# Attention, layer norm and a float32 feed-forward on one core: the first pass's stores begun from GpSimd's queue, the residual stored in token order

## The chip, the cores and the metric

The kernel runs on one core of a Trainium2 chip. The metric is the device time of one execution in microseconds (us); the median of several runs is compared. TensorE is written PE, VectorE DVE, ScalarE ACT, GpSimd POOL and SyncE SP. A DMA is begun by an instruction on the queue of one of these engines (SP, ACT, or POOL) and then runs by itself.

## What is computed

```python
# q, k, v: (8, 8, 576, 64) float32; x below is (8, 576, 512), heads side by side
q_d, k_d, v_d = mean over each 4 tokens            # 144 pooled tokens
out_up  = repeat(softmax(scale * q_d @ k_d.T) @ v_d, 4)          # pooled attention
out_loc = softmax(scale * q @ k.T where |i - j| < 4) @ v         # local attention
x  = out_up + out_loc
xn = (x - mean(x)) / sqrt(var(x) + 1e-6) * g_ln                  # over 512 columns
return x + relu(xn @ w_ch1) @ w_ch2                              # 512 -> 2048 -> 512
```

The weights arrive as 8-byte floats, which the kernel reads as pairs of 32-bit words and turns into float32 itself. Each float32 product of the feed-forward is made of three faster ones, from a high and a low part of either operand.

## The kernel before

**Work.** The 4608 tokens of the 8 batches are cut in two ways. Attention goes by *windows*: window `i` (40 in all, 5 to a batch) holds two rows of 58 queries (56 in a batch's last window), `par` 0 and 1, each inside a stretch of 64 rows. The feed-forward goes by *chunks* of 512 tokens, 9 in all. Its 2048 hidden columns are split in two sets: a first pass visits all 9 chunks with the first set (5 pairs of 256 columns, plain products, line 1224 up and 1295 down), a second pass visits them again with the second set (3 pairs, a form with 7 products for 8, line 1214 up). Attention and norm of all windows run beside the first pass, so the first pass is where loads, pooling and norms are; the second pass has only the feed-forward.

**What goes through DRAM.** The first pass stores four things. `ud` (line 963): pooled attention of half the heads of a batch, each row written 4 times, 2 DMAs, read back by windows as `up` (line 1021). `xs` (line 1091): the residual x of a window, as it stands in SBUF, all 128 rows with the overlap of the windows, 1 DMA. `blocks` (line 1131): the normalised, transposed operand of a chunk, 4 DMAs, read back in the second pass (line 1146). `parts` (line 1364): the first pass's share of the output, 128 tokens to a DMA, after ACT has evicted it from PSUM (line 1361). In the second pass `fetch` brings `xs` and `parts` back for 128 tokens at a time; since `xs` lies by windows, the 128 rows are put together from 2 to 4 DMAs (line 1388), `parts` from one (line 1385). POOL adds the two (line 1391), DVE adds the second pass's share out of PSUM (line 1394), SP stores the result (line 1399).

**The engines beside PE.** POOL pools raw q, k and v over 4 tokens (lines 827 and 828: `raw5q` gives half of `qd`; 5 is 2 times the batch plus the half of the heads), adds `up` to the window's local attention (line 1040), takes a power for the norm (line 1053), and in the second pass makes sums of operands (line 1165) and line 1391. The raw tiles have two buffers in all, so a load waits until POOL has pooled the one before the last. PE turns `qd` and `kd` (line 875), makes pooled scores (902), turns the exponentials (921) and multiplies by the pooled v (938). SP begins the loads: raw tiles (line 814), windows of q and k in blocks (561, 4 DMAs to a task), windows of v (578 and 584), weights (359, 364). A block load of q or k may be given to ACT's queue instead (`alt` in `local`, windows from 16 on).

**The order.** Every piece of work is a task of a planner (`Plan`): an engine, a cost in us, what it depends on, a due time, and the buffers it takes and gives. `Plan.order` lists all tasks by a forecast of times and the kernel then emits them in that order, so each engine's instructions stand in a fixed order and an instruction that waits holds up all behind it on its engine. The planner counts at most 8 DMAs in flight (`lanes`) for all queues together. Costs, leads and due times are numbers in the kernel (`W_NORM`, `W2_LATER`, `DB` and others): when one changes, the order of every engine can change.

## Time and profile before

| what | value |
|---|---|
| median of 3 runs | 1067.28 us (1064.33 to 1073.89) |
| the profiled execution | 1064.17 us |
| its span, first to last instruction | 1062.5 us |
| mean granted clock of PE, as a share of full speed | 0.988 |
| instructions | 22984 |
| moved by DMA | 160.28 MB |

The profiled execution took 1064.17 us, of which 1062.5 us are the span; 1.7 us lie around it. Busy times are sums over an engine's instructions. Matmuls overlap and their ends are modelled, so a PE that is busy all the time can still be slowed; where PE stands still the timeline gives the idle time before an instruction in square brackets, with what ended it. "SPq" and "ACTq" rows are DMA-issuing instructions on a queue, with the time they took to issue; the transfer itself follows. Each row of a timeline is an instruction, or several equal ones in a row (x4), with start and length. The granted clock is 1.00 at 2.4 GHz and 0.50 at 1.2 GHz.

### The profile page before, as it was taken

What the parts mean: (1) busy time and instruction counts of PE and PEld (TensorE: products, weight loads), DVE (VectorE), ACT (ScalarE), POOL (GpSimd) and SP (SyncE); (2) the same over time, 40 slices, a digit from 0 to 9 for tenths busy, and PEclk for the clock granted to TensorE, in tenths of its full rate; (3) what the DMA queues carried; (4) which work ended last, traced back from release to release, by engine and by line L of the source; (5) the groups of instructions that cost most, each with busy time, mean ns of one, the idle gap of its engine ahead of it and who ended that gap; (6) DMA issues with size and microseconds to landing.
All of it is one profiled execution on the core that took longest, in us unless ns stands there. A gap on an engine that the chain in (4) does not pass through costs nothing. (4 is left out here: it accounts for less than half of the span.)

```text
span 1062.5 us, 22984 instructions
## 1 busy us (share of the span) xinstructions
PE 1021.6 (96%) x8330; PEld 861.6 (81%) x8330; DVE 663.7 (62%) x1573; ACT 434.7 (41%) x1352; POOL 363.8 (34%) x358
## 2 busy tenths in 40 slices
PE   9899999898999899999999999999998999999998
PEld 8678777777777688878888887888888999988897
DVE  6899874675565375655665554654646775466574
ACT  6686743362442354244453452553323223222221
POOL 4343454443534543352320111220213244214422
PEclk9999999999999999999999999999999999999999
DMA  7999877768787857667556242431345333433433
GB/s 177 226 270 243 205 171 164 185 164 177 165 174 177 190 132 188 139 171 186 144 136 167 75 132 81 139 120 55 105 128 170 103 108 108 159 124 105 131 118 119
DMA packets 284930, 160.28 MB, mean 151 GB/s; under 512 B 194704, under 2 KB 248080, under 8 KB 284816
## 3 DMA queue, kind: packets, MB, share of 16 engines
q1 hardware_dynamic: 263056, 156.18, 55.5%
q10 hardware_dynamic: 21760, 2.63, 1.7%
q8 instruction: 66, 1.08, 0.4%
q14 instruction: 48, 0.39, 0.1%
HBM read 111.68 MB, written 47.05 MB: 149 GB/s over the span
## 5 line engine op out<-in xcount | busy, mean ns | idle before, releaser
L1295 PE MATMUL acc<-hiw,hl 128*128 128x512 f32 x576 | 236.3, 410 | 4.9 <-ACT s L1252 2.5
L1295 PE MATMUL acc<-low,hh 128*128 128x512 f32 x576 | 226.5, 393 | 0.0
L1295 PE MATMUL acc<-hiw,hh 128*128 128x512 f32 x576 | 226.3, 393 | 0.0
L1295 PEld LDWEIGHTS acc<-hiw,hl 128*128 128x128 f32 x576 | 109.2, 190 | 27.8 <-ACT s L1252 3.1
L1295 PEld LDWEIGHTS acc<-hiw,hh 128*128 128x128 f32 x576 | 108.9, 189 | 24.3
L1232 ACT ACTIVATE hh<-h 128x256 fp32r<-128x256 f32 x180 | 59.6, 386 | 163.5 <-PE h L1224 99.9
L1295 PEld LDWEIGHTS acc<-low,hh 128*128 128x128 f32 x576 | 109.5, 190 | 17.4
L1391 POOL TENSOR_TENSOR back<-back,back 128x512 f32<-128x512 f32 x36 | 49.4, 1404 | 193.1 <-DMA back<-parts 170.1
L1239 DVE SCALAR_TENSOR_TENSOR hl<-h,hh 128x256 fp32r<-128x256 f32 x180 | 67.2, 414 | 76.6 <-ACT hh L1232 75.6
L1224 PE MATMUL h<-hix,hiw 128*128 128x512 f32 x360 | 111.0, 404 | 0.0
L1224 PE MATMUL h<-hix,low 128*128 128x512 f32 x360 | 103.1, 407 | 2.2 <-DVE low L408 0.8
L1224 PE MATMUL h<-lox,hiw 128*128 128x512 f32 x360 | 97.8, 394 | 0.0
L1040 POOL TENSOR_TENSOR xl<-xl,up 128x512 f32<-128x512 f32 x35 | 45.2, 1297 | 145.1 <-DVE xl L749 27.9
L1224 PEld LDWEIGHTS h<-lox,hiw 128*128 128x128 f32 x360 | 68.2, 189 | 15.2
L1224 PEld LDWEIGHTS h<-hix,low 128*128 128x128 f32 x360 | 65.7, 191 | 16.2 <-ACT hix L402 1.9
L1275 ACT ACTIVATE hh<-e 128x256 fp32r<-128x256 f32 x108 | 38.3, 408 | 97.2 <-DVE e L1256 55.5
L1224 PEld LDWEIGHTS h<-hix,hiw 128*128 128x128 f32 x360 | 65.5, 190 | 12.7
L1088 ACT ACTIVATE xg<-px,gain 128x58 f32<-128x58 f32 (+15 forms) x280 | 61.7, 380 | 6.9 <-PE px L1065 6.7
L1281 DVE SCALAR_TENSOR_TENSOR hl<-e,hh 128x256 fp32r<-128x256 f32 x108 | 54.3, 554 | 8.1 <-ACT hh L1275 7.1
L1256 DVE TENSOR_TENSOR e<-h,s 128x512 f32<-128x512 f32 x27 | 18.5, 684 | 47.7 <-PE h L1214 40.7
L1214 PE MATMUL h<-hiT,los 128*128 128x256 f32 x216 | 44.2, 287 | 3.6 <-ACT part L1361 3.0
L938 PEld LDWEIGHTS gv<-vd,agt 72*72 72x72 f32 x512 | 38.4, 146 | 9.8 <-ACT agt L931 3.6
(237 smaller groups left out, 1951.3 us busy)
## 6 DMA issues: line engine op xcount, KB each, us to landing
s<-in_moe_w_ch_dram SPq DMA_DIRECT2D x64, 256.0 KB
xs<-xl SPq DMA_DIRECT2D x40, 256.0 KB
blocks<-xg SPq DMA_DIRECT2D x36, 256.0 KB
parts<-part SPq DMA_DIRECT2D x36, 256.0 KB
xf_B<-blocks SPq DMA_DIRECT2D x36, 256.0 KB
back<-parts SPq DMA_DIRECT2D x36, 256.0 KB
out_dram<-back SPq DMA_DIRECT2D x36, 256.0 KB
up<-ud SPq DMA_DIRECT2D x70, 128.0 KB
```

The lines of the kernel that those rows point to most:

```text
L938: nc.tensor.matmul(y.pv[:, qh, h2], lhsT=y.at[kh][:, h2, qh * GH : (qh + 1) * GH], rhs=vd[:, kh, 2 * pr + h2], start=kh == 0, stop=kh == 1,)
L1040: nc.gpsimd.tensor_add(xl(), xl(), x.up)
L1088: nc.scalar.activation(to, at, AF.Copy, scale=gain[:, kc : kc + 1])
L1214: nc.tensor.matmul(side(*PLACE[e]), lhsT=wt[:, k], rhs=xx[:, k], start=n == 0, stop=n == 5)
L1224: nc.tensor.matmul(y.ps[fi], lhsT=wt[a][:, kc * P : (kc + 1) * P], rhs=xx[b], start=n == 0, stop=n == 3 * KC - 1)
L1232: nc.scalar.activation(hh[v, p, th][:, 256 * fi : 256 * fi + 256], side(fi, th), AF.Relu)
L1239: nc.vector.scalar_tensor_tensor(out=hl[v, p, th][:, fs], in0=side(fi, th), scalar=0.0, in1=hh[v, p, th][:, fs].bitcast(F32), op0=ALU.max, ...
L1256: nc.vector.tensor_add(two(y.e1), two(y.ps[1]), both(y.s))
L1275: nc.scalar.activation(hh[v, p, th][:, 256 * fi : 256 * fi + 256], place(th, fi), AF.Relu)
L1281: eng.scalar_tensor_tensor(out=hl[v, p, th][:, fs], in0=place(th, fi), scalar=0.0, in1=hh[v, p, th][:, fs].bitcast(F32), op0=ALU.max, op1= ...
L1295: nc.tensor.matmul(acc[v, th][j], lhsT=lt[:, ts], rhs=rt, start=p == 0 and fi == 0 and n == 0, stop=p == npr - 1 and fi == 1 and n == 2,)
L1391: nc.gpsimd.tensor_add(y.x, y.x, y.p)
```

## The change

The stores `ud`, `xs`, `blocks` and `parts` are begun on POOL's queue instead of SP's. `xs` is laid out by tokens: a window's store is cut into its two rows of queries (2 DMAs of 58 or 56 rows, without the overlap), and `fetch` reads 128 tokens with one DMA. The planner counts DMAs in flight that POOL began apart from the others (`soft`), and gives a start on POOL a cost (`BEGUN`). Five numbers of the planner change with it: `W_NORM`, `W2_LATER`, `DB`, and the costs of the loads of q, k and v by SP. The number of tasks stays.

```diff
@@ Plan.order
-                    if len(self.landed) >= self.lanes:
-                        at = max(at, self.landed[-self.lanes])
+                    landed = self.soft if t.eng == "POOL" else self.landed
+                    if len(landed) >= self.lanes:
+                        at = max(at, landed[-self.lanes])
+                    if t.eng == "POOL":
+                        at += t.dur / t.pieces
...
-    W_NORM, G_NORM = 4.0, 9.0
+    W_NORM, G_NORM = 2.0, 9.0
-    W2_LATER = 4.0
+    W2_LATER = 7.0
+    BEGUN = 1.0
-                    ts.append(add("SP", 1.9, lambda src=src, nm=nm, jb=jb: load_blocks(src, nm, jb, nc.sync), ts,
+                    ts.append(add("SP", 1.95, lambda src=src, nm=nm, jb=jb: load_blocks(src, nm, jb, nc.sync), ts,
-        vt = add("SP", 2.65 if by_pe else 1.33, load_v, (last_local.v[i % NVW],), due - 8.0, lag=LAT, kb=360,
+        vt = add("SP", 2.75 if by_pe else 1.42, load_v, (last_local.v[i % NVW],), due - 8.0, lag=LAT, kb=360,
@@ keep (ud), in pooled_pair
-                nc.sync.dma_start(
+                nc.gpsimd.dma_start(
-        t = add("SP", 0.74, keep, x.od_done, due, lag=LAT, kb=640, n=2, more=0.6)
+        t = add("POOL", 2 * BEGUN, keep, x.od_done, due, lag=LAT, kb=640, n=2, more=0.6)
-    xs = dram.tile([B * NWIN, P, DM], F32, tag="xs", bufs=1, name="xs")
+    xs = dram.tile([NT, DM], F32, tag="xs", bufs=1, name="xs")
@@ spill (xs), in norm
-            nc.sync.dma_start(xs[i], xl())
+            for par in range(2):
+                q0, n = queries(i, par)
+                r0 = row_of(i, par)
+                nc.gpsimd.dma_start(xs[q0 : q0 + n], xl()[r0 : r0 + n])
-        spilled[i] = add("SP", 0.41, spill, (t, kept), due + 2.0, give=U, lag=LAT, kb=256)
+        spilled[i] = add("POOL", 2 * BEGUN, spill, (t, kept), due + 2.0, give=U, lag=LAT, kb=256, n=2, more=2.0)
@@ save (blocks), in operands
-                    nc.sync.dma_start(blocks[c, kc], block[c, kc])
+                    nc.gpsimd.dma_start(blocks[c, kc], block[c, kc])
-                block_done[c, kc, "saved"] = add("SP", 0.41, save, [t], due + 10.0, give=U, lag=LAT, kb=256)
+                block_done[c, kc, "saved"] = add("POOL", BEGUN, save, [t], due + 10.0, give=U, lag=LAT, kb=256)
-    DB = 5.4
+    DB = 5.8
@@ finish: parts and the way back
-                nc.sync.dma_start(parts[n], y.p)
+                nc.gpsimd.dma_start(parts[n * P : (n + 1) * P], y.p)
-                for i, r0, r, m in pieces:
-                    nc.sync.dma_start(t[r : r + m], xs[i, r0 : r0 + m])
+                nc.sync.dma_start(t, src[n * P : (n + 1) * P])
-                parted[n] = add("SP", 0.41, keep, (t,), due + 1.0, give=U, lag=LAT, kb=256)
+                parted[n] = add("POOL", BEGUN, keep, (t,), due + 1.0, give=U, lag=LAT, kb=256)
```

**What it moves.** SP's instructions, at the loads of the raw tiles of batch 2's second half of heads (`raw5`). Before, stores of `ud` and `xs` stand between the loads (`qr`, `kr` are block loads of q and k):

```order
L561 DMA qr_2361<-in_q_dram 32x8x32 x4
L963 DMA ud_2492<-od_2403 288x1x256 x2
L814 DMA raw5q_2497<-in_q_dram 72x4x256
L561 DMA kr_2407<-in_k_dram 32x8x32 x4
L814 DMA raw5k_2535<-in_k_dram 72x4x256
L561 DMA qr_2545<-in_q_dram 32x8x32 x4
L1091 DMA xs<-xl_1451 128x512
L1091 DMA xs<-xl_1638 128x512
```

After, at the same loads, SP has loads alone:

```order
L819 DMA raw5q_2599<-in_q_dram 72x4x256
L566 DMA kr_2511<-in_k_dram 32x8x32 x4
L583 DMA vwin_79<-in_v_dram 64x8x64 x2
L566 DMA qr_2684<-in_q_dram 32x8x32 x4
L566 DMA kr_2726<-in_k_dram 32x8x32 x4
L819 DMA raw5k_2774<-in_k_dram 72x4x256
L819 DMA raw5v_2776<-in_v_dram 72x4x256
```

The stores have left SP, and the load of `raw5v` stands right behind that of `raw5k`. Over the whole program SP loses 36 + 36 + 40 + 28 stores and 76 of the 112 pieces of the way back, and gains 40 block loads that ACT had: 1135 instructions become 959.

POOL's instructions at the same place. Before, the second halves of `raw5q` and `raw5k` are pooled one after the other:

```order
L1053 TENSOR_TENSOR mv_2489<-mv_2489,neg_half 128x1
L827 TENSOR_TENSOR raw5q_2497<-raw5q_2497 72x4x128
L828 TENSOR_TENSOR qd_2429<-raw5q_2497 72x256
L827 TENSOR_TENSOR raw5k_2535<-raw5k_2535 72x4x128
L828 TENSOR_TENSOR kd_2476<-raw5k_2535 72x256
L827 TENSOR_TENSOR raw5v_2640<-raw5v_2640 72x4x128
```

After, eight starts of stores stand between them:

```order
L832 TENSOR_TENSOR raw5q_2599<-raw5q_2599 72x4x128
L833 TENSOR_TENSOR qd_2508<-raw5q_2599 72x256
L1099 DMA xs<-xl_1662 58x512 x2
L1099 DMA xs<-xl_1886 58x512 x2
L1099 DMA xs<-xl_2223 58x512 x2
L1139 DMA blocks<-xg_0_1220 128x512
L1139 DMA blocks<-xg_1_1222 128x512
L832 TENSOR_TENSOR raw5k_2774<-raw5k_2774 72x4x128
L833 TENSOR_TENSOR kd_2681<-raw5k_2774 72x256
```

Each start stands behind whatever its tile waits for, and `kd` behind them all. Over the whole program POOL gets 180 starts (80 `xs`, 36 `blocks`, 36 `parts`, 28 `ud`) to its 363 instructions.

ACT's instructions near the second product of batch 3's second half of heads. Before, a block load stands between the exponentials `ag` and the copy `agt` of their transpose:

```order
L915 ACTIVATE ag_1_4048<-gs_1_4005,gmx_1_4031 96x144 x3
L561 DMA qr_4085<-in_q_dram 32x8x32 x4
L931 COPY agt_1_0_4130<-gt_1_0_4098 72x3x2x48
L931 COPY agt_1_1_4134<-gt_1_1_4105 72x3x2x48
```

After, the nearest block load stands between two halves of a relu of the feed-forward:

```order
L936 COPY agt_0_1_3984<-gt_0_1_3965 72x3x2x48
L1240 ACTIVATE hh_0_0_4003<-h_0_0_3935 128x256
L1240 ACTIVATE hh_0_1_4005<-h_0_0_3935 128x256
L566 DMA qr_4041<-in_q_dram 32x8x32 x4
L1240 ACTIVATE hh_0_0_4003<-h_0_1_4009 128x256
```

The 20 block loads that ACT begins (80 DMAs) become 10 (40 DMAs).

## Rows read from the trace of the kernel before

**Rows 1.** The page: busy time of each engine, its share of the span, and the number of instructions.

```profile
PE 1021.6 (96%) x8330; PEld 861.6 (81%) x8330; DVE 663.7 (62%) x1573; ACT 434.7 (41%) x1352; POOL 363.8 (34%) x358
```

**Rows 2.** What PE waited for: instruction and line, released by; us in total, times, longest.

```profile
PE gq L875 <- POOL kd L828: 4.2, 3, 1.7
PE lt L706 <- ACT la L697: 3.5, 2, 2.4
PE gv L938 <- ACT agt L931: 3.1, 1, 3.1
PE gt L921 <- ACT ag L915: 3.1, 2, 1.7
PE h L1214 <- ACT part L1361: 3.0, 1, 3.0
PE gv L938 <- POOL vd L828: 2.2, 2, 1.6
```

**Rows 3.** Busy time by engine in the seven stretches where the granted clock was 0.50 (columns: stretch, length, busy PE, PEld, DVE, ACT, POOL, clock, DMA share, GB/s).

```profile
153.10:156.50 3.40, 3.40 (x21) 2.68 (x12) 2.09 (x6) 3.39 (x13) 0.00 (x0) 0.50 0.65 131
197.50:200.80 3.30, 3.30 (x11) 2.61 (x11) 1.73 (x6) 0.95 (x4) 0.00 (x0) 0.50 0.26 44
262.40:265.70 3.30, 3.30 (x41) 2.75 (x40) 2.91 (x11) 0.00 (x0) 0.00 (x0) 0.50 0.97 185
327.20:330.50 3.30, 3.30 (x13) 2.62 (x12) 0.76 (x2) 1.35 (x4) 0.00 (x0) 0.50 0.89 206
368.20:371.50 3.30, 3.30 (x38) 2.27 (x37) 0.00 (x0) 1.77 (x6) 2.00 (x3) 0.50 0.96 287
457.00:460.20 3.20, 3.20 (x11) 2.46 (x9) 0.77 (x2) 0.91 (x3) 0.00 (x0) 0.50 0.74 204
805.10:808.40 3.30, 3.11 (x14) 3.11 (x15) 3.30 (x7) 0.90 (x3) 0.00 (x0) 0.50 0.57 194
```

**Rows 4.** SP's queue in order of time, 140 to 175 us: start, us, what.

```profile
140.64 1.72 SPq L963 DMA_DIRECT2D ud<-od  x2
142.46 0.57 SPq L814 DMA_DIRECT2D raw5q<-in_q_dram  x1
143.08 2.71 SPq L561 DMA_DIRECT2D kr<-in_k_dram  x4
145.89 0.36 SPq L814 DMA_DIRECT2D raw5k<-in_k_dram  x1
...
167.98 4.22 SPq L1364 DMA_DIRECT2D parts<-part  x2
...
174.34 0.36 SPq L814 DMA_DIRECT2D raw6q<-in_q_dram  x1
```

**Rows 5.** PE in order of time: two instructions before which it stood still, with the idle time and what ended it.

```profile
152.34 0.28 PE L875 MATMUL gq<-ident,kd 72*128 72x72 f32 x1 [1.75 <-POOL kd L828]
...
805.29 0.80 PE L1214 MATMUL h<-hiT,los 128*128 128x256 f32 x2 [3.02 <-ACT part L1361]
```

**Rows 6.** The four stores on SP's queue, by line: count, ns to issue one (min/median/max), first and last start in us.

```profile
L1364 SPq DMA_DIRECT2D parts<-part x36: 319/356/580, 168.0 to 806.0; - x36
...
L1091 SPq DMA_DIRECT2D xs<-xl x40: 319/405/1430, 42.2 to 678.7; - x40
...
L963 SPq DMA_DIRECT2D ud<-od x28: 810/840/895, 74.6 to 615.4; - x28
...
L1131 SPq DMA_DIRECT2D blocks<-xg x36: 319/394/530, 65.8 to 691.7; - x36
```

**Rows 7.** The block loads that ACT's queue begins, in the same form.

```profile
L561 ACTq DMA_DIRECT2D qr<-in_q_dram x48: 317/328/1332, 166.3 to 453.6; - x48
L561 ACTq DMA_DIRECT2D kr<-in_k_dram x32: 317/330/1237, 218.2 to 572.2; - x32
```

**Rows 8.** ACT in order of time around three of them: start, us, what, and the idle time before it with what ended it.

```profile
258.90 1.88 ACTq L561 DMA_DIRECT2D qr<-in_q_dram  x4
260.83 0.69 ACT L931 COPY agt<-gt 72x288 f32<-72x288 f32 x2 [9.36 <-DMA kr<-in_k_dram]
...
300.04 0.91 ACT L915 ACTIVATE ag<-gs,gmx 96x144 f32<-96x144 f32 x3 [8.31 <-DMA qr<-in_q_dram]
...
324.90 0.66 ACT L1232 ACTIVATE hh<-h 128x256 fp32r<-128x256 f32 x2 [6.81 <-DMA qr<-in_q_dram]
```

**Rows 9.** Busy time by engine in a long stretch of the first pass (columns as in rows 3).

```profile
100.00:300.00 200.00, 184.91 (x1667) 150.64 (x1666) 131.44 (x346) 88.11 (x294) 94.39 (x93) 0.97 0.79 177
```

**Rows 10.** POOL's groups of instructions, its longest over a whole tile and its smallest: count, busy us, mean ns, idle before with what ended it.

```profile
L1391 POOL TENSOR_TENSOR back<-back,back 128x512 f32<-128x512 f32 x36 | 49.4, 1404 | 193.1 <-DMA back<-parts 170.1 <-DMA xf_B<-blocks 23.0
...
L1053 POOL TENSOR_TENSOR mv<-mv,neg_half 128x1 f32<-128x1 f32 x40 | 22.5, 571 | 44.3 <-DVE mv L1050 38.4 <-DMA s<-in_moe_w_ch_dram 5.8
```

**Rows 11.** What SP's queue waited for: the reads of the second pass (1385 `parts`, 1146 `blocks`, 1388 `xs`).

```profile
SPq L1385 <- DMA back<-xs: 28.2, 17, 2.9
...
SPq L1146 <- DMA back<-xs: 18.0, 10, 2.8
SPq L1388 <- DMA back<-xs: 15.8, 11, 2.6
```

**Rows 12.** POOL in order of time in the second pass.

```profile
957.60 5.49 POOL L1391 TENSOR_TENSOR back<-back,back 128x512 f32<-128x512 f32 x4 [22.98 <-DMA back<-parts]
963.04 1.29 POOL L1165 TENSOR_TENSOR xT<-xf_B,xf_B 128x512 f32<-128x512 f32 x1
```

More of the change, by code (lines that the diff above doesn't have):

```diff
@@ L39, in __init__ @@
         self.wire, self.lanes = 1.05, 8
-        self.landed = []
+        self.landed, self.soft = [], []
     def add(self, eng, dur, fn, deps=(), due=0.0, take=(), give=(), lag=None, ahead=1e9, alt=None, kb=0, n=1, more=0.1, late=None):
@@ L125, in order @@
                 for _ in range(t.pieces):
-                    if len(self.landed) >= self.lanes:
-                        at = max(at, self.landed[-self.lanes])
+                    landed = self.soft if t.eng == "POOL" else self.landed
[3 more added lines that the diff above has]
+                        at += t.dur / t.pieces
                     self.moved = max(self.moved, at + self.wire) + t.kb / t.pieces / self.rate
-                    self.landed.append(self.moved + t.more)
-                    last = max(last, self.landed[-1])
-                    at += t.dur / t.pieces
+                    landed.append(self.moved + t.more)
+                    last = max(last, landed[-1])
+                    if t.eng != "POOL":
+                        at += t.dur / t.pieces
                 t.end = at
@@ L179, in attention_then_ffn @@
     NT = B * S
-    NTILE = NT // P
     TPC = 2 * T // P
@@ L991, in pooled_pair @@
             return
-        t = add("SP", 0.74, keep, x.od_done, due, lag=LAT, kb=640, n=2, more=0.6)
+        t = add("POOL", 2 * BEGUN, keep, x.od_done, due, lag=LAT, kb=640, n=2, more=0.6)
         ud_done.setdefault(b, []).append(t)
     block, block_done, spilled = {}, {}, {}
-    xs = dram.tile([B * NWIN, P, DM], F32, tag="xs", bufs=1, name="xs")
-    parts = dram.tile([NTILE, P, DM], F32, tag="parts", bufs=1, name="parts")
+    xs = dram.tile([NT, DM], F32, tag="xs", bufs=1, name="xs")
+    parts = dram.tile([NT, DM], F32, tag="parts", bufs=1, name="parts")
     blocks = dram.tile([NCH, KC, P, 512], F32, tag="blocks", bufs=1, name="blocks")
@@ L1363, in keep, with fetch @@
             def keep(y=y, n=n):
-                nc.sync.dma_start(parts[n], y.p)
-            pieces = []
-            t, r = n * P, 0
-            while r < P:
-                for i in range(B * NWIN):
-                    for par in range(2):
-                        q0, m = queries(i, par)
-                        if q0 <= t < q0 + m:
-                            m = min(q0 + m - t, P - r)
-                            pieces.append((i, row_of(i, par) + t - q0, r, m))
-                            t, r = t + m, r + m
-                            if r == P:
-                                break
-                    if r == P:
-                        break
-            def fetch(y=y, n=n, src=None, pieces=pieces):
+                nc.gpsimd.dma_start(parts[n * P : (n + 1) * P], y.p)
+            near = [
+                i for i in range(B * NWIN) for par in range(2)
+                if queries(i, par)[0] < (n + 1) * P and sum(queries(i, par)) > n * P
+            ]
+            def fetch(y=y, n=n, src=None):
                 t = unit([P, DM], f"back{n}")
                 setattr(y, "p" if src is parts else "x", t)
-                if src is parts:
-                    nc.sync.dma_start(t, src[n])
-                    return
-                for i, r0, r, m in pieces:
-                    nc.sync.dma_start(t[r : r + m], xs[i, r0 : r0 + m])
+                nc.sync.dma_start(t, src[n * P : (n + 1) * P])
             def both(y=y):
@@ L1402, in finish @@
                 t = add("ACT", act(512), evict, (done,), due, take=U, give=A)
-                parted[n] = add("SP", 0.41, keep, (t,), due + 1.0, give=U, lag=LAT, kb=256)
+                parted[n] = add("POOL", BEGUN, keep, (t,), due + 1.0, give=U, lag=LAT, kb=256)
                 continue
             back = [
-                add("SP", 0.41 * k if k == 1 else 0.75 * k, lambda y=y, n=n, src=src, fetch=fetch: fetch(y, n, src), t, due - 6.0,
-                    take=U, lag=LAT, kb=256 * min(k, 2), n=k, more=0.1 if k == 1 else 2.0, ahead=10.0)
-                for src, t, k in ((xs, [spilled[e[0]] for e in pieces], len(pieces)), (parts, [parted[n]], 1))
+                add("SP", 0.41, lambda y=y, n=n, src=src, fetch=fetch: fetch(y, n, src), t, due - 6.0,
+                    take=U, lag=LAT, kb=256, ahead=10.0)
+                for src, t in ((xs, [spilled[i] for i in near]), (parts, [parted[n]]))
             ]
```

## The prediction

> **What bounds the kernel now.** I read the page first. PE is busy for 1021.6 of 1062.5 us [rows 1]. The kernel is bound by PE, and no change to stores can win more than the time in which PE stands still or runs slowly. So the next views are PE's waits, its clock, and from each wait back to what came late.
>
> PE's waits [rows 2] fall into three kinds. (a) The copy `kd` and the pooled v of POOL: 4.2 + 2.2 = 6.4 us. (b) ACT's results `la`, `agt` and `ag`: 3.5 + 3.1 + 3.1 = 9.7 us. (c) In the second pass the 3.0 us before line 1214 at 805.29 [rows 5]. The clock adds to it: in seven stretches it was granted at 0.50, which is 1.2 GHz, 6 x 3.3 + 3.2 = 23.0 us together [rows 3]. PE worked in them at half speed, so each cost half its length, some 1.7 us. The first begins just after PE's idle time before 152.34, the last during the wait that ends at 805.29 [rows 3, 5]. I put the first two down to kind (a), the four from 262 to 457 us to kind (b), where ACT was held for long just before (until 260.83 and 324.90 [rows 3, 8]), and the last to kind (c): 3.4, 6.8 and 1.7 us. With their clock the kinds cost 9.8, 16.5 and 4.7 us, 31 us in all. That is the most that can be won there, 3%.
>
> Where do (a) and (b) come from? SP's queue in order of time shows DMA starts back to back: 140.64 + 1.72 ends at 142.36 and the load of `raw5q` starts at 142.46, then block loads until 145.79 and `raw5k` at 145.89 [rows 4]. That `raw5k` becomes the `kd` for which PE waits at 152.34 [rows 5]. Ahead stand 1.72 us of `ud` stores; ahead of the `raw6q` at 174.34 stand 4.22 us for two stores of `parts` [rows 4]. SP is full here, and what is late for PE is late because SP began it late. ACT's waits tell the same of kind (b): before `agt` at 260.83 it stood 9.36 us, before `ag` at 300.04 8.31 us, before a relu at 324.90 6.81 us, each time behind a block load of its own queue [rows 8]. ACT has such loads, 48 + 32 DMAs [rows 7], since SP has no room for them.
>
> **The change part by part.** The sum is made against the profiled execution, 1064.17 us (1062.5 of span and 1.7 around it). It is the fastest of its kernel's times; the median of the three runs is 3.1 us above it, and that goes on again at the end.
>
> *Stores leave SP.* 36 x 0.356 + 40 x 0.405 + 28 x 0.840 + 36 x 0.394 = 12.8 + 16.2 + 23.5 + 14.2 = 66.7 us of issuing, between 42.2 and 806.0 us [rows 6], nearly all in the first 700. None of it was on PE's path by itself; its worth is in what SP begins earlier.
>
> *Block loads leave ACT.* The order shows 20 of them before and 10 after, and the one between `ag` and `agt` is gone from there. Kind (b) cost 16.5 us [rows 2, 3]. Bounds: 0, if the ten that stay are those that hurt, and -16.5, if none does. I take the half, -8.2, by the halved count.
>
> *Raw loads come earlier.* Kind (a), 9.8 us [rows 2, 3]. Bounds: 0 if POOL is then late instead, -9.8 if the waits go. The 1.72 us of stores ahead of `raw5k` are as long as the 1.75 us that PE waited [rows 4, 5], but eight starts now stand ahead of that `kd` on POOL, so not all goes: -6.
>
> *Starts on POOL.* 180 of them. The trace of before has none, so the price is bounded by the nearest rows: below, an SP start of the same 256 KB, 0.36 us [rows 6]; above, POOL's longest pass over such a tile, 1.40 us [rows 10]. (The smallest POOL instruction, 0.57 us, lies between [rows 10].) I take the middle, 0.9 us: 162 us. About 180 x 200 / 764 = 47 of them fall between 100 and 300 us, 42 us on top of 94.39 us of POOL's work in these 200 [rows 9]: 137 of 200, and 111 or 160 at the two ends. The cover is POOL's idle time. It holds on average, but not in every place: the store waits for its tile on POOL's queue (`xs` for the norm, `blocks` for DVE's low part, `parts` for ACT's eviction), and behind it are queued the poolings for which PE waits, and the raw loads that need their two buffers back. Bounds 0 and +20 (rival 2); I take +3, about one wait of 1.75 us with its clock.
>
> The Trainium skill has a price for this path, in the page "DMA: Bandwidth & Descriptors", section "Latency and other measured facts": about 1 us to the first byte for a DMA begun by GpSimd, against about 0.6 us from the hardware path. No row of before shows it; as 180 x 1.0 us it would be an estimate of 180 us, and the sum would be the same within 1 us.
>
> *The way back.* SP waited 28.2 + 18.0 + 15.8 = 62 us behind the pieces of `xs` [rows 11], which become 36 whole tiles instead of 112 pieces. These waits reach PE through POOL: `xT` at 963.04 stands behind 5.49 us of additions that began after 22.98 us of waiting for the read of `parts` [rows 12], and operands that come late like this end in kind (c). Bounds 0 and -4.7; I take -3, the wait without its clock.
>
> *Numbers of the planner.* `W_NORM`, `W2_LATER`, `DB` and the costs move tasks by a few places; PE has the same instructions but for fillers. Priced at 0; the cover is that PE is busy for 96% of the span [rows 1] with work that no due time makes longer. Without the cover a shift costs what a wait of [rows 2] costs, up to 3 us with its clock, either way.
>
> Sum: -8.2 - 6 + 3 - 3 = -14.2, so 1064.2 - 14.2 = 1050.0 for an execution like the profiled one, and + 3.1 = 1053 for the median, 1.3% under 1067.28. The last result is stored from SP as before: the end of the span does not change.
>
> **The rivals.**
>
> 1. *All waits go.* With SP free, ACT's ten loads no longer wait for SP's buffers, and (a), (b) and (c) vanish: 1067.3 - 9.8 - 16.5 - 4.7 = 1036. For it: all three have SP behind them. Against: every removed wait of PE shows the next one, and eight starts before `kd` are a new one.
>
> 2. *POOL becomes the late supplier (slower).* Place: `kd` and `vd` of batches 2 to 7, between 100 and 500 us, where POOL is at 94 of 200 us [rows 9] and gets 47 starts. Price: in each half of a batch a wait as at 152.34, 1.75 us, and 1.7 us of clock: 3.45 us; in six of the twelve halves 20.7 us. Kind (a) isn't won; -8.2 and -3 stay: 1067.3 - 11.2 + 20.7 = 1077. It decides from about 1.4 us a start, where 160 of 200 us are taken and stores wait in order besides. For it: fixed order, and stores that wait for their producers. Against: in before POOL stood waiting for loads, so it has slack in front of the poolings.
>
> 3. *The transfers are the limit (no change).* The DMA engines were busy at 0.79 from 100 to 300 us [rows 9]. If loads land late because bytes wait, not starts, (a) and (b) stay and the starts cost 3, the way back wins 3: 1067. Against: SP's starts stand back to back, and a store's bytes move just the same. The Trainium skill, page "DMA: Bandwidth & Descriptors", section "Issuing engines are not separate DMA queues", speaks for this rival: starting DMAs from several engines saves only the sequencer's time to start them, usually small. Rows 4 and 6 agree that it is starting time that is saved, and disagree that it is small here: 66.7 us of a full queue.
>
> 4. *The change doesn't do what it says*, since SP fills up with the block loads from ACT: 40 x 0.33 us [rows 7] are 13 us of the 66.7 that it lost. It is too little to fill it; no chance of its own.
>
> **How the numbers follow.** Forecast 0.50 (its own range 1045 to 1062: the halves taken in its terms, 8 us to either side), all waits gone 0.13, POOL late 0.17, transfers the limit 0.20. About 1% (1056.6 and 1078.0) is what a measurement tells from no change. Faster: 0.42 of the forecast and 0.13 = 0.55. Same: 0.08 of the forecast, 0.20, and 0.02 of rival 2 = 0.30. Slower: the rest of rival 2, 0.15. The range goes from rival 1 to the price of rival 2: 1037 to 1076.
>
> **What would show it.** Right: SP's queue has gaps between 100 and 500 us; fewer and shorter waits of ACT behind its own loads; fewer than seven stretches at 0.50; the waits of PE for `kd`, `vd`, `agt`, `ag` and `la` under 9 us together against 16.1; POOL's starts near 0.9 us. Wrong: PE waits longer for `kd` and `vd` than 6.4 us, with a DMA start just ahead of them on POOL (rival 2); waits as before with SP idle (rival 3); or starts on POOL outside 0.36 to 1.40 us.

## The result and the profile after

The median after is 1035.01 us (1032.09 to 1038.76, 4 runs), before, timed beside it, 1065.80 us. The ratio is 0.971, with a 95% interval of 0.964 to 0.978: 31 us, where 14 were forecast. It is below the range, at the price of rival 1. The profiled execution after took 1032.09 us, its span 1030.4 us. For two kernels further below, one run over 1.5% above the fastest of its kernel is left out of the median.

Lines of the changed kernel: 832 and 833 pool, 968 `ud`, 1099 `xs`, 1139 `blocks`, 1372 `parts`, 1382 the way back, 566 block loads, 819 raw loads, 880 to 943 pooled attention, 1232 and 1303 the first pass, 1222 the second.

The page, to be held against [rows 1]:

```profile
PE 1008.4 (98%) x8332; PEld 854.5 (83%) x8332; DVE 664.1 (64%) x1559; ACT 449.3 (44%) x1408; POOL 463.2 (45%) x538
```

PE stands still for 1030.4 - 1008.4 = 22.0 us; before it was 1062.5 - 1021.6 = 40.9. So 19 us of the 32 between the spans are waits. Another 8 are the clock: seven stretches at 0.50 with 23.0 us [rows 3] have become one of 6.8 us, and half of the difference is lost work. The 5 us that are left lie inside PE's busy time, and no row shows what they are. What PE waited for, against [rows 2]:

```profile
PE acc L1303 <- DVE low L413: 5.0, 2, 3.8
PE gt L926 <- ACT ag L920: 2.7, 3, 1.9
PE gs L907 <- ACT ktg L893: 1.9, 2, 1.4
PE lq L216 <- POOL ident masks.py:199: 1.8, 1, 1.8
PE gq L880 <- POOL kd L833: 1.4, 1, 1.4
PE gv L943 <- POOL vd L833: 1.3, 1, 1.3
```

Kind (a) fell from 6.4 to 2.7 us, kind (b) from 9.7 to 2.7, and the wait of kind (c) is gone. A new one leads, 5.0 us on `low`, and the only low clock within the work begins during it, at 135.5 us: busy time by engine in the two halves of that stretch (columns as in [rows 3]).

```profile
135.50:138.90 3.40, 1.28 (x3) 1.08 (x4) 2.07 (x1) 0.00 (x0) 3.32 (x4) 0.50 1.10 180
138.90:142.30 3.40, 3.40 (x13) 3.06 (x13) 0.67 (x2) 1.19 (x2) 2.54 (x3) 0.50 0.34 50
```

By stage, before (first fence) and after (second), in the same columns:

```profile
150.00:325.00 175.00, 160.42 (x1415) 130.01 (x1413) 102.43 (x279) 72.42 (x256) 77.14 (x77) 0.97 0.76 172
325.00:500.00 175.00, 169.41 (x1452) 137.68 (x1453) 101.94 (x286) 67.79 (x231) 76.11 (x77) 0.97 0.74 173
675.00:1060.00 385.00, 376.04 (x2180) 332.00 (x2179) 232.35 (x402) 120.31 (x301) 111.71 (x86) 1.00 0.37 120
```

```profile
150.00:325.00 175.00, 169.50 (x1547) 138.84 (x1546) 111.03 (x305) 89.39 (x314) 115.07 (x141) 1.00 0.81 191
325.00:500.00 175.00, 175.00 (x1573) 143.55 (x1572) 109.75 (x300) 77.90 (x269) 105.07 (x126) 1.00 0.70 165
675.00:1030.00 355.00, 350.58 (x2075) 312.06 (x2073) 218.86 (x373) 105.15 (x255) 107.53 (x87) 1.00 0.35 121
```

PE's idle time falls from 14.6 to 5.5 us between 150 and 325, from 5.6 to none up to 500, and from 9.0 to 4.4 in the second pass. POOL carries 29 to 38 us more in either stretch of the first pass and PE is better fed all the same. The first product of the form that only the second pass has starts 22.2 us earlier than before:

```profile
L1214 PE MATMUL h<-hiT,los x216: 277/283/583, 744.9 to 1045.8; 128*128 128x256 f32 x108
```

```profile
L1222 PE MATMUL h<-hiT,los x216: 277/283/388, 722.7 to 1014.1; 128*128 128x256 f32 x108
```

So 22 of the 32 us between the spans are won ahead of the second pass, where the forecast's terms (-8.2, -6 and +3) come to 11, and 10 us within it, where it had 3.

The price of a start on POOL, in its groups of instructions (count, busy us, mean ns, idle before and what ended it), where the forecast had 900 ns:

```profile
L1099 POOL DMA_DIRECT2D xs<-xl x80 | 44.6, 563 | 0.0
...
L968 POOL DMA_DIRECT2D ud<-od x28 | 20.4, 751 | 43.1 <-DVE od L962 37.9 <-DVE hl L1247 5.2
L1372 POOL DMA_DIRECT2D parts<-part x36 | 20.2, 565 | 48.8 <-ACT part L1369 38.6 <-ACT ag L920 9.7 <-issue 0.2
L1139 POOL DMA_DIRECT2D blocks<-xg x36 | 19.8, 557 | 22.5 <-ACT xg L1093 22.5
```

105 us for 180 starts, 0.58 us each. In the stretch of [rows 9] POOL's work comes to 131 us, where the forecast had 137:

```profile
100.00:300.00 200.00, 191.40 (x1742) 158.39 (x1744) 140.86 (x359) 98.07 (x333) 131.06 (x154) 0.98 0.81 188
```

POOL does stand waiting in front of stores (37.9, 38.6 and 22.5 us above), and PE's waits for `kd` and `vd` shrank all the same. SP's queue in order of time, against [rows 4]:

```profile
140.43 1.88 SPq L566 DMA_DIRECT2D kr<-in_k_dram  x4
142.41 0.36 SPq L819 DMA_DIRECT2D raw5k<-in_k_dram  x1
...
150.85 1.94 SPq L566 DMA_DIRECT2D kr<-in_k_dram  x4
157.46 0.31 SPq L819 DMA_DIRECT2D raw5k<-in_k_dram  x1
159.53 0.31 SPq L819 DMA_DIRECT2D raw5v<-in_v_dram  x1
```

There are gaps now, from 152.79 to 157.46 and from 157.77 to 159.53. SP's last block load starts at 566.9 us, before at 591.0.

### The profile page after: what moved, and what is told of

The parts are those of the page before. It is cut to its first block, busy times and chain, and to the rows that moved or that the text cites. A ratio compares the mean times of both kernels' runs of the same rounds, so it can differ in the third digit from the quotient of the medians.

```text
span 1030.4 us, 23083 instructions
## 1 busy us (share of the span) xinstructions
PE 1008.4 (98%) x8332; PEld 854.5 (83%) x8332; DVE 664.1 (64%) x1559; ACT 449.3 (44%) x1408; POOL 463.2 (45%) x538
## 5 line engine op out<-in xcount | busy, mean ns | idle before, releaser
L1289 DVE SCALAR_TENSOR_TENSOR hl<-e,hh 128x256 fp32r<-128x256 f32 x108 | 57.0, 578 | 5.2 <-PE acc L1303 3.4
L1058 POOL TENSOR_TENSOR mv<-mv,neg_half 128x1 f32<-128x1 f32 x40 | 23.9, 601 | 47.6 <-DVE mv L1055 38.7
L1099 POOL DMA_DIRECT2D xs<-xl x80 | 44.6, 563 | 0.0
```

The lines of the kernel that those rows point to most:

```text
L1058: nc.gpsimd.tensor_tensor(x.mv[:, 1:2], x.mv[:, 1:2], neg_half, op=ALU.pow)
L1099: nc.gpsimd.dma_start(xs[q0 : q0 + n], xl()[r0 : r0 + n])
L1289: eng.scalar_tensor_tensor(out=hl[v, p, th][:, fs], in0=place(th, fi), scalar=0.0, in1=hh[v, p, th][:, fs].bitcast(F32), op0=ALU.max, op1= ...
```

## The experiments

Four theories were to be told apart. SP: what gained is that SP begins loads earlier. Layout: it is `xs` in the order of tokens. Numbers or order: it is the new order. POOL late: a store in POOL's order holds what PE needs. "Same order" below means that the instructions of PE, DVE and ACT stand as in the kernel named, apart from DMA starts on ACT. All ratios are to the kernel before, timed beside it, with 95% intervals in brackets; what a run won or lost against before is worked out from the ratio.

### The parts of the change, with the planner told

**The five numbers alone**, on the kernel before.

```diff
-    W_NORM, G_NORM = 4.0, 9.0
+    W_NORM, G_NORM = 2.0, 9.0
```

and W2_LATER 7.0, DB 5.8, SP's costs 1.95, 2.75 and 1.42.

> The kernel before (1065.8 us) with only the five numbers of the planner changed (W_NORM 2, W2_LATER 7, DB 5.8, the two costs of SP's tasks); stores stay on SP and xs keeps its windows. Theory SP (the gain is SP's freed starting time): 1066 within 8, since SP issues just as many DMAs, and ACT still issues about 80 block loads. Rival numbers (the order that the numbers bring is what gains): 1040 to 1050, and PE's waits for kd, vd, agt and ag shrink from about 16 us towards 8 without any start leaving SP.

Measured: 1063.33 us, ratio 0.998 (0.995 to 1.001). By themselves the numbers gain nothing that can be told from none.

**Stores on POOL, planner told, old layout and numbers.**

```diff
-                nc.sync.dma_start(blocks[c, kc], block[c, kc])
+                nc.gpsimd.dma_start(blocks[c, kc], block[c, kc])
```

and so for `ud`, `xs` (one DMA) and `parts`, with the planner's lines of the change.

> The kernel before with the stores begun from GpSimd's queue and planned there, but xs still in windows (one store a window, read back in two or more pieces) and the old numbers. Theory SP: the gain of the first pass is here, 18 to 23 us of the 31, so 1043 to 1048; the second pass keeps its lane waits behind the pieces of back (PE stalls there about 9 us, as before). Rival layout: 1058 to 1066, since the pieces stay.

Measured: 1059.49 us, 0.992 (0.990 to 0.995). These 8 us are less than theory SP said and lie in the range of rival layout, but they are more than nothing. In the order of before the same stores on POOL win 14 us (below), so the order that the planner makes once it knows of them loses some 6 us again.

**Layout alone, stores on SP.**

```diff
-            nc.sync.dma_start(xs[i], xl())
+            for par in range(2):
+                nc.sync.dma_start(xs[q0 : q0 + n], xl()[r0 : r0 + n])
```

and the plain `fetch` of the change.

> The kernel before with xs in the order of tokens, stored by two DMAs from SP and read back as plain tiles, all stores still on SP, old numbers. Theory SP: only the second pass gains, 1056 to 1062: its stalls fall from about 9 us to about 2, the first pass stays (40 more SP starts there). Rival layout: 1040 to 1048, the greater part of the gain.

Measured: 1143.65 us, 1.072 (1.068 to 1.075): 76 us slower. Both theories were wrong, and this became the question of the third group. SP's queue, and below it the busy times (columns as in [rows 3]) while it starts nine halves of `xs` in a row:

```profile
254.99 11.47 SPq L1094 DMA_DIRECT2D xs<-xl  x9
266.54 5.37 SPq L561 DMA_DIRECT2D kr<-in_k_dram  x4
```

```profile
255.00:267.00 12.00, 11.86 (x61) 8.67 (x61) 5.95 (x13) 11.98 (x51) 3.01 (x4) 1.00 0.27 83
267.00:278.00 11.00, 6.08 (x67) 4.77 (x65) 0.00 (x0) 2.05 (x6) 0.00 (x0) 1.00 0.26 68
```

SP is stuck, 1.3 us to a start, with the DMA engines busy at 0.27. Neither starting time nor bytes explain that.

**The kernel after with the old five numbers.**

```diff
-    W2_LATER = 7.0
+    W2_LATER = 4.0
```

and the other four.

> The kernel after (1035.0 us) with the old five numbers. Theory SP: 1035 to 1042; PE's 5 us wait for the low words of the first w2 and the 6.8 us of half clock behind it near 137 us should be gone with W2_LATER at 4, others of 1 to 3 us may come. Rival numbers: 1050 or more, since the order that they tune is lost.

Measured: 1051.80 us, 0.985 (0.982 to 0.988). With the stores on POOL the numbers are worth 0.014 of the time, 15 us, near what rival numbers said.

### One thing moved, same order

Where two kernels have the same order on PE, the starts of the same PE instruction in the two traces can be compared: the lead of one over the other shows where time is won. Ahead of the first instruction that the edit moves, it came to 5 us in one of these traces and to a lag of up to 13 us in another. A difference of that size between two single executions proves nothing.

**Only the queue of the stores**, order of before.

```diff
-                nc.sync.dma_start(parts[n], y.p)
+                nc.gpsimd.dma_start(parts[n], y.p)
```

and so for `xs`, `ud` and `blocks`; the planner still counts them on SP.

> The order of before on PE, DVE and ACT, word for word; only the stores (xs, ud, blocks, parts: one xs store a window as before) are begun from POOL's queue, at the places where the planner had put them on SP. ACT still issues its 80 block loads, and xs is read back in pieces. Theory SP (a free SP brings loads earlier): PE's waits for kd and vd go, those for agt, ag and la stay; 1052 to 1060. Rival order (what gains is the order that the planner makes with the new costs, not the queue): 1063 to 1070. Rival POOL late: a store that waits for its data in POOL's order holds kd, vd and xl behind it: 1070 or more.

Measured: 1053.43 us, 0.987 (0.984 to 0.990), 14 us by the queue alone. What PE waited for:

```profile
PE h L213 <- ACT la L697: 5.9, 1, 5.9
PE gt L921 <- ACT ag L915: 3.6, 1, 3.6
PE gq L875 <- POOL kd L828: 3.3, 2, 1.7
```

`vd` and `agt` are no longer in the list, `kd` is 3.3 against 4.2, and `la` and `ag` are there with 9.5 us as against 6.6. Kind (a) shrank by 3.1 us, PE's idle time by 8.3 us in all (1049.6 - 1017.0 = 32.6 against 40.9): the gain comes also out of small waits that no row of [rows 2] holds. The lead is 12.1 us at 770 us and 12.7 at the end, so it is won in the first pass. Whether it is SP's starting time that counts, or its waits for earlier DMAs to land, this run doesn't tell.

**All stores of after back on SP**, order of after.

```diff
-                nc.gpsimd.dma_start(xs[q0 : q0 + n], xl()[r0 : r0 + n])
+                nc.sync.dma_start(xs[q0 : q0 + n], xl()[r0 : r0 + n])
```

and so for the other three.

> The order of after on PE, DVE and ACT, word for word; only its stores (80 xs halves, 28 ud, 36 blocks, 36 parts) are begun from SP again, at their places in the plan. Theory SP: most of the gain goes, 1058 to 1085, with PE waits for kd, vd, vwin back, since SP holds 180 more starts and its lanes are shared with stores of 58 rows. Rival order: within 10 us of after (1035 to 1045), since the order alone made the gain.

Measured: 1140.82 us, 1.068 (1.065 to 1.071), 106 us over after. Rival order falls: the same order without the free queue is worse than before. But 180 starts do not cost 106 us either.

**Only ACT's block loads**, order of before.

```diff
-  lambda ...: load_blocks(src, nm, jb, nc.scalar)
+  lambda ...: load_blocks(src, nm, jb, nc.gpsimd)
```

> The order of before on PE, DVE and ACT; its stores stay on SP; only the 80 block loads that ACT issues (31.9 us of ACT's time, 28 gaps of 121.5 us in which ACT did nothing else) are begun from POOL's queue. If the term Block loads leave ACT is right, the waits for agt, ag and la (9.7 us) and the half clock behind them go: 1052 to 1060. If ACT's loads were late for another reason (data of the blocks late, not ACT held), no change: 1063 to 1069. POOL pays 80 starts of about 0.56 us.

Measured: 1057.71 us, 0.990 (0.987 to 0.994). ACT's groups (count, busy us, mean ns, idle before and what ended it), of before and then of this kernel:

```profile
L1232 ACT ACTIVATE hh<-h 128x256 fp32r<-128x256 f32 x180 | 59.6, 386 | 163.5 <-PE h L1224 99.9 <-DMA qr<-in_q_dram 23.9 <-DMA kr<-in_k_dram 14.1
...
L931 ACT COPY agt<-gt 72x288 f32<-72x288 f32 x64 | 22.9, 420 | 33.2 <-PE gt L921 18.4 <-DMA kr<-in_k_dram 13.5 <-PE gv L938 1.1
```

```profile
L1232 ACT ACTIVATE hh<-h 128x256 fp32r<-128x256 f32 x180 | 59.8, 386 | 152.3 <-PE h L1224 141.0 <-issue 8.9 <-DMA xs<-xl 2.1
...
L931 ACT COPY agt<-gt 72x288 f32<-72x288 f32 x64 | 22.9, 417 | 29.3 <-PE gt L921 28.9 <-PE gv L938 0.3 <-ACT agt L931 0.2
```

The parts of the idle time that ended with a load, 23.9 + 14.1 and 13.5 us, are gone, and ACT waits for PE in their place: ACT was held by its own loads, as the prediction took it. PE's waits for `la` and `ag` are 3.2 and 2.6 us and `agt` is out of the list, 5.8 us in place of 9.7, so not all of kind (b) came from these loads. This execution was 8.7 us behind before at 166 us, where ACT's first such load stood, and 3.4 us ahead at the end: 12 us won from there on.

**Only the pieces of the way back**, order of before.

```diff
-                    nc.sync.dma_start(t[r : r + m], xs[i, r0 : r0 + m])
+                    nc.gpsimd.dma_start(t[r : r + m], xs[i, r0 : r0 + m])
```

> The order of before; only the 112 pieces of the way back (back<-xs, 6 to 58 rows) are begun from POOL, everything else as before. On SP a piece of 58 rows landed after 7.3 us at the median, and SP waited 62 us for its lanes behind pieces in the second pass; stores of 58 rows from POOL landed after 3.1 us. Theory narrow: PE's stalls of the second pass (9.5 us) and its half clock (1.7 us) mostly go: 1055 to 1060. The forecast's term: 3 us, 1062 to 1063. Rival POOL late: POOL's own additions wait behind pieces that wait for a free tile, 1066 or more.

Measured: 1052.21 us, 0.986 (0.981 to 0.990), 15 us (10 to 21) where the forecast had 3. Not all of it is the pieces' doing. Before, the first of them starts at 772.3 us:

```profile
L1388 SPq DMA_DIRECT2D back<-xs x112: 224/307/1936, 772.3 to 1041.3; - x112
```

At 770 us, with the same program up to there, this kernel's profiled execution already led by 5.1 us, and at the end by 15.8. So 10.7 us are shown to come from the pieces, three and a half times the forecast. The second pass (columns as in [rows 3]):

```profile
675.00:1045.00 370.00, 367.39 (x2158) 326.33 (x2156) 223.37 (x392) 117.37 (x292) 162.48 (x196) 1.00 0.38 123
```

PE's idle time is 2.6 us there, before 9.0, and no clock of 0.50 but the one at the end of the span is left. SP's list of waits has no row on `back<-xs` any more. POOL's share grows by 51 us in this pass, without harm. On SP the 58-row pieces landed after 7.3 us at the median, and the 128-row reads of `parts` among them after 7.7; with the pieces on POOL the two took 2.5 and 4.6 us. SP is rid of 112 starts and of their narrow shape at once here, and no run of the second pass tells the two apart.

**The three together**, stores, ACT's loads and pieces, in the order of before.

> The order of before on PE, DVE and ACT; the stores, ACT's 80 block loads and the 112 pieces of the way back are all begun from POOL; xs keeps its windows, and the planner knows of none of it. If the parts add up: 1066 less 13, 10 and 14, 1026 to 1033. If stores and ACT's loads share one gain (both bring the first pass its loads earlier, and POOL holds 248 starts), 1034 to 1043. If the new order of the change is needed: 1045 or more.

Measured: 1037.44 us, 0.976 (0.971 to 0.982), 25 us, with 332 DMAs begun on POOL (140 + 80 + 112, not 248). The three share a part of their gain (14 + 10 + 15 singly), as the middle expectation said. The lead over before is 19.5 us at 770 us and 30.2 at the end: 10.7 us for the pieces again. The new layout, the order and the numbers are not needed for the greater part of what the change brings.

### Why 58 rows are slow from SP

**Only the halves of `xs` on SP**, order of after, by the one line shown above; the other 100 stores stay on POOL.

> The order of after; of its stores only the 80 halves of xs (64 of 58 rows, 16 of 56) are begun from SP, the 100 others stay on POOL. On SP a 58-row store landed in 7.4 us at the median with 3 updates of its semaphore in the trace, a 128-row one in 2.9 us with 16. Theory narrow (a 58-row DMA from SP runs on few DMA engines and holds SP's lanes and the loads behind it): 1085 to 1130, the greater part of the 106 us that all the stores on SP cost. Rival starts (only SP's starting time counts): 80 starts of 0.3 to 0.5 us, 1035 + 24 to 40 at most, 1045 to 1075.

**The same, each half in two DMAs.**

```diff
+                for a, z in ((0, 48), (48, n)):
+                    nc.sync.dma_start(xs[q0 + a : q0 + z], xl()[r0 + a : r0 + z])
```

> As the run with the halves of xs on SP, but each half in two DMAs, of 48 rows and of the 10 or 8 left: 160 starts on SP in place of 80, the same bytes. Theory narrow: 48 rows and 10 rows spread over more engines than 58 do (a read of 16 rows showed 16 updates, one of 58 three), so it is faster than the unsplit one by 20 us or more although SP starts 80 DMAs more: 1060 to 1095. Rival starts: 25 to 40 us slower than the unsplit one.

Measured: 1123.47 us, 1.055 (1.051 to 1.059), and split 1062.90 us, 0.998 (0.995 to 1.001). Twice as many starts on SP are 60 us faster. Rival starts falls, theory narrow holds. With the unsplit halves PE is level with after at 50 us, 44 us behind at 250 and 91 at 600, and loses nothing more: all the loss falls into the first pass. From each start to the last update of its semaphore in the trace, medians by shape, worked out from the records of updates:

| rows of 2 KB | begun by | updates | us to the last |
|---|---|---|---|
| 58 (unsplit) | SP | 3 | 7.1 |
| 56 (unsplit) | SP | 15 | 3.2 |
| 48 (split) | SP | 16 | 2.6 |
| 10 (split) | SP | 11 | 1.9 |
| 58 (after) | POOL | 16 | 3.1 |

A store of 58 rows takes longer than one of 128 rows on the same queue before, 2.85 us with 16 updates. The Trainium skill has the rule in the page "DMA: Bandwidth & Descriptors", section "Why a DMA increments its semaphore by 16 and not by 1": a DMA from SP runs on the largest number of DMA engines up to 16 that divides its outermost dimension, only these count up its semaphore, and the sequencer writes the rest at once. The trace agrees: 58 gives 2 and one write, 56 gives 14 and one, 48 gives 16, 10 gives 10 and one. The section also has an exception for GpSimd's path, which spreads some copies by rounding up; on POOL 58 rows land in 3.1 us, but the number of engines that they used no run here shows.

What PE waited for with the halves on SP:

```profile
PE gq L880 <- POOL kd L833: 17.7, 4, 10.9
PE lq L604 <- DMA qn<-in_q_dram: 13.4, 2, 11.7
PE gv L943 <- POOL vd L833: 12.3, 2, 11.0
```

`kd`, `vd` and `qn` come from loads that SP begins among the narrow stores. Before, pieces of the way back were such narrow DMAs: 36 of the 112 have 58 rows, and they took 7.3 us.

### What is left, and a faster kernel

**W2_LATER alone put back to 4, and W_NORM alone put back to 4**, on the kernel after.

> The kernel after with W2_LATER back at 4 and the other four numbers kept. If the wait of 5 us for the low words of the first w2 near 133 us, and the 6.8 us at half clock behind it, come from W2_LATER 7, they go: 1027 to 1033, faster than after by 2 to 8 us. Rival: the four numbers work only together, and other waits come in the first 300 us: 1036 to 1052.

> The kernel after with W_NORM back at 4 and the four other numbers kept. If W_NORM carries the numbers' gain (16 us for all five), 1045 to 1052. If the numbers gain by the chance of an order (W2_LATER alone, put back, cost 8 us), any other time of 1035 to 1055, with its waits at other places of the first 300 us than the run with W2_LATER at 4 has.

Measured: 1043.25 us (0.978, 0.974 to 0.982) and 1042.94 us (0.977, 0.971 to 0.983). What PE waited for, in the first and then in the second:

```profile
PE gq L880 <- POOL kd L833: 8.1, 2, 4.4
PE gt L926 <- ACT ag L920: 5.3, 2, 4.9
```

```profile
PE h L1232 <- DVE low L413: 2.5, 3, 1.3
PE gq L880 <- POOL kd L833: 2.2, 1, 2.2
PE gv L943 <- POOL vd L833: 1.8, 1, 1.8
```

The wait on `low` went with W2_LATER, and others took its place. Both intervals overlap that of after (0.964 to 0.978), so 8 us for one number alone is not sure. Four orders of one mechanism gave 1035 to 1052 us, with their waits at different places. That fits the rival of a chance of order; that the numbers chosen suit this order for a reason isn't shown.

**ACT's loads of after on POOL, and then the raw loads too**, order of after.

> The order of after; its 40 block loads that ACT issues (19.2 us of ACT's time) are begun from POOL's queue. Before lost 9.6 us with its 80 loads off ACT; theory: what is left of that term goes, 3 to 5 us, 1029 to 1033. Rival: ACT has slack by now, and POOL's queue makes them later: 1035 to 1040.

> As the run before, and the 84 raw loads too are begun from POOL, whose own additions free and use their buffers; SP has 84 starts (40 us) less. Theory SP (what is left of PE's waits in the first 500 us is SP's starting time): 1020 to 1028. Rival POOL late: a raw load stands in POOL's order behind stores that wait for ACT and DVE, so kd and vd come later: 1036 or more.

Measured: 1031.40 us, 0.968 (0.963 to 0.972), 4 us under after, inside what was expected though the intervals overlap; and 1054.53 us, 0.990 (0.984 to 0.995). Taking still more from SP gives 23 us back. That is the time of rival POOL late; at which place it is lost isn't shown.

**The hold near 131 us.** DVE and POOL of the kernel after, in order of time:

```profile
129.82 7.75 DVE L413 TENSOR_TENSOR low<-cva,hiw 128x512 fp32r<-128x512 f32 x2
```

```profile
132.08 4.93 POOL L1045 TENSOR_TENSOR xl<-xl,up 128x512 f32<-128x512 f32 x4
```

The second of the two `low` begins at 131.46 and lasts 6.11 us, until 0.6 us after the fourth addition; the median of all 26 is 0.68 us. PE waits 3.8 us for it, and the slow clock begins during that wait. In the kernel with ACT's loads on POOL another DVE instruction of two operands, the first of the two `cva` here, lasts 5.75 us beside the same additions, until 0.3 us after the fourth:

```profile
130.61 6.08 DVE L387 SCALAR_TENSOR_TENSOR cva<-s,cva 128x256 int32<-128x256 int32 x2
```

```profile
131.13 4.95 POOL L1045 TENSOR_TENSOR xl<-xl,up 128x512 f32<-128x512 f32 x4
```

Two runs on top of ACT's loads on POOL, the first with

```diff
             nc.gpsimd.tensor_add(xl(), xl(), x.up)
+            if NWIN <= i < NWIN + 4:
+                nc.gpsimd.tensor_copy(pause, xl()[:, :1])
```

> The kernel after with ACT's loads begun from POOL (1031.4 us), and after each of the four additions xl+up of windows 5 to 8 one POOL copy of a 128x1 column that reads the sum. Its PE waits 5.7 us near 132 us for low words that DVE makes; a DVE instruction there lasts 5.7 us (0.6 usually) while POOL runs four additions in a row (131.13 to 136.08). Theory hold (a row of POOL additions without a gap holds DVE's two-operand instruction until it ends): the break lets DVE through, the wait and the 6.8 us of half clock behind it shrink: 1022 to 1028. Rival: DVE waits for something else, 1030 to 1034.

and the second with these four additions on DVE:

```diff
-            nc.gpsimd.tensor_add(xl(), xl(), x.up)
+            eng = nc.vector if NWIN <= i < NWIN + 4 else nc.gpsimd
+            eng.tensor_add(xl(), xl(), x.up)
```

> As the run before, without the copies: the four additions are done by DVE, at their places in the order. Theory hold: four additions of about 0.6 us on DVE in place of a hold of 5 us: 1021 to 1028. Rival: the additions wait for up on DVE and hold its low words as long, 1030 to 1036.

Measured: 1035.14 us, 0.970 (0.965 to 0.974), and 1021.88 us (1019.20 to 1027.71), 0.958 (0.952 to 0.964). The first is above both expectations and settles nothing: in its profiled execution the additions came at 140 to 146 us, away from `low`, whose wait is gone, while other waits (`vd` 3.2, `kd` 2.2 us) cost as much. The second is the fastest of all, 13 us under after; in its DVE rows the two `low` take 1.28 us and the additions follow, and no DVE instruction from 126 to 150 us lasts over 1.4 us.

```profile
134.12 1.28 DVE L413 TENSOR_TENSOR low<-cva,hiw 128x512 fp32r<-128x512 f32 x2
135.32 1.28 DVE L1046 TENSOR_TENSOR xl<-xl,up 128x512 f32<-128x512 f32 x2
```

The first 150 us (columns as in [rows 3]), first of the run with the same loads and the additions on POOL, then of this one:

```profile
0.00:150.00 150.00, 138.52 (x1669) 115.57 (x1670) 128.18 (x299) 95.36 (x298) 74.47 (x99) 0.95 0.86 214
```

```profile
0.00:150.00 150.00, 142.65 (x1721) 119.62 (x1722) 127.84 (x314) 97.64 (x308) 72.57 (x98) 0.99 0.87 212
```

PE's idle time falls by 4.1 us and its mean clock rises from 0.95 to 0.99. Not all of the clock is the additions' doing: with them on POOL one stretch at 0.50 lies at 36.5 to 43.3 us, long before them. At the same PE instruction the run with the additions on DVE is 2.3 us behind at 131 us and 5.4 ahead at 145: 7.6 us are won at this place, of 9.5 between the two medians.

## Why the prediction was wrong

The mechanism was right, the sum too small: three of its terms were mis-sized. The numbers of the planner stood at 0 and are worth 15 us here; the way back stood at -3, with a bound of -4.7, and won 11; stores and raw loads stood at -6 + 3, with a bound of -9.8, and won 14 by themselves. The time ended at that of rival 1, all waits go, which got a chance of 0.13. That is partly luck, for not all the named waits went.

**The bound.** The prediction took 31 us for "the most that can be won there". That was the sum over six rows of [rows 2], 19 us, with their clock. PE stood still for 40.9 us [rows 1], and 22 us of that were in other rows, mostly smaller. Of the six rows 5.4 us are left after the change, so 13.7 went; the others lost 10, and the new wait on `low` took 5.0 back. When supply gets earlier the small waits shrink as well, so a term bounded by its named rows is bounded too low.

**Stores leave SP; raw loads come earlier; starts on POOL.** Forecast -6 and +3, measured 14 us won when only the queue moves. The gain exceeds the bound of 9.8 us, for the reason above. The price of a start was mis-sized, 0.9 us against 0.58, and so was its harm: POOL does wait in front of stores (37.9, 38.6 and 22.5 us), and `kd` and `vd` together fell to 2.7 us all the same.

**Block loads leave ACT.** Forecast -8.2, measured -10 in the order of before when all 80 leave. In after 40 stay, and moving these wins some 4 us more, so the change's part is near 6. This term held.

**The way back.** This step failed by most against its own bound: -3 with a bound of -4.7, measured -11 in two runs (15 by the medians of the one that moved only the pieces). The prediction read 62 us of SP's waits behind pieces [rows 11], and followed them to one wait of PE; PE's idle time in the second pass was 9.0 us, and its low clock there cost 1.7 more. It took the pieces for many starts, and not for slow ones. Before, a read of 58 rows took 7.3 us, the 36 whole tiles in their place take 4.4. How much of the 11 us comes of the shape and how much of the count stays open. For the stores the shape is shown: it is why the layout needs the other queue, and with its stores on SP it costs 76 us.

**Numbers of the planner.** Priced at 0. That is right for the kernel before (0.998) and wrong after, where the old ones cost 15 us. This is the one term that accounts for the miss by itself: without the new numbers the kernel after takes 1051.80 us, and the forecast, which gave them nothing, said 1053. The cover named, a busy PE, says nothing on how long the waits become in another order; the bound of 3 us was for one wait, and an order moves many. That the rest of the sum came out at 1052 is luck in part: its terms were too small, and the planner's own order for the stores lost some of the gain again (8 us in place of 14). Why these five numbers suit this order stays open.

**Transfers as the limit** (rival 3) falls: the DMA share from 100 to 300 us is 0.81 against 0.79 in [rows 9], and the time went down. The rule that the prediction set beside it, from the Trainium skill, page "DMA: Bandwidth & Descriptors", section "Issuing engines are not separate DMA queues", says that starting DMAs from several engines saves only the time to start them, usually small. No run here contradicts the first half; moving 140 starts alone won 14 us, so it was not small here.

**The signs that were named.** Gaps in SP's queue: there. Low clock in fewer than seven stretches: one within the work. Waits for `kd`, `vd`, `agt`, `ag` and `la` under 9 us: 5.4. Starts near 0.9 us: no, 0.58. ACT waits less behind its own loads, as one of its groups shows, 15.9 us against 23.9 + 14.1:

```profile
L1240 ACT ACTIVATE hh<-h 128x256 fp32r<-128x256 f32 x180 | 59.4, 386 | 144.9 <-PE h L1232 127.5 <-DMA qr<-in_q_dram 15.9 <-issue 1.3
```

The three moves measured singly come to more than the three together (39 us against 25), since they share gains, so these figures don't add up to an account of the 31 us to the microsecond.

## What to carry to other kernels

When a DMA queue is full, look at each transfer's shape before its count: a row count with few divisors can hold the queue for longer than several plain transfers, and cutting it in two can be faster. Bound a gain in supply by all of the critical engine's idle time and not by the named waits. Test a reordering change with the order held still, one queue at a time; four orders from nearby numbers differed here by 1.6%. And look where the time is won: of 15.8 us between two executions, 5.1 were there before the moved instructions began.

## What the runs showed of the hardware

- From SP, a store of 58 rows of 2 KB took 7.1 us with 3 updates, one of 48 rows 2.6 us with 16; from POOL 58 rows took 3.1 us.
- A DMA start on POOL took 0.56 us for 56 to 128 rows of 2 KB and 0.75 us for the `ud` store that writes each row four times. For the same stores SP took 0.84 us for `ud` [rows 6].
- A DVE instruction with two operands in SBUF lasted 6.11 us in place of 0.68 beside four POOL additions in a row, and ended 0.6 us after them; with ACT's loads on POOL another lasted 5.75 us and ended 0.3 us after them. Both began during the pooling of `vd` just ahead. With the additions on DVE none there was held. In the run with the break DVE's norm statistics, with one operand, took their usual 0.69 us beside the same additions. Whether a gap between the additions would let DVE through no run shows.
